# Seven sparse hops on one core: blocks gathered and scattered in pairs, fetches in fours, token scaling on ScalarE

## The chip, the core and the metric

One core of a Trainium2 chip runs the whole program. Its engines work side by side, each through its own queue in order, and wait for each other on semaphores: TensorE (PE in the profile, its weight loads PEld) for matrix products into PSUM, VectorE (DVE) and ScalarE (ACT) for elementwise work and for copies out of PSUM, GpSimd (POOL), which here mostly issues gathers by index from memory, and SyncE (SP), which issues plain transfers. The metric is the device time of one execution in microseconds. The kernel before takes 3991.62 us (median of 3 runs, 3988.89 to 3995.74).

## What is computed

A graph with 10,000 nodes, 160,000 edges and rows of 128 numbers. Seven hops each sum, for every node, the scaled rows of its neighbours; the eight rows that a node then has (its own and one of each hop) go through a small attention layer.

```python
h = x
toks = [x]
for _ in range(7):
    msg = h[src] * deg_inv_sqrt[src, None] * deg_inv_sqrt[dst, None]
    h = _segment_sum(msg, dst, N)
    toks.append(h)
tok = jnp.stack(toks, axis=1)                      # (N, 8, D)
...
return jnp.einsum('nk,nkd->nd', alpha, o)
```

The change lies in hops 2 to 7. The sorting of the edges, hop 1 and the attention keep their code.

## The kernel before

**Tables.** The rows of a hop stand in SBUF as a table `tab` of 80 tiles of 128 nodes, each row in two halves of fp16 (a value and its remainder, 256 columns together). There are two such tables, and hops read one and write the other. The written rows also go to memory (`tabd`, and `tabh` for tiles 72 to 78), because a part of the edges is fetched from there.

**Blocks.** The nodes that receive are cut into 79 tiles; the work for one is a block. What it needs of the edges was made once in hop 1: a matrix `w` of 128 x 4736 fp8 ones and zeros, which every hop loads again from memory (`GSd`, line 695, on SP). Its columns are 72 gather matrices of 32 columns, 18 scatter matrices of 128 columns and one matrix for fetched rows. Tiles 72 to 78 come first in a hop, then 0 to 71 (`order`).

**Gather (`gather`, lines 533 to 543).** A tile `p` in PSUM takes eight matmuls (line 539): 32 columns of `w` against one tile of the table each, so that four of them, on four groups of 32 columns of the array, make 128 rows of 256 sums. Nine such tiles, jj = 0 to 8, make a block. A copy (line 542) brings each as fp16 into a buffer `eb`: ScalarE copies jj = 0, 2, 4, 5, 7, VectorE 1, 3, 6, 8 (`evac`). The pool of `p` has six banks (`pg2`), and there are 14 buffers `eb`.

**Scatter (`scat`, lines 510 to 519).** Two matmuls per tile (line 515), 128 columns of `w` against a buffer `eb`, add up into the block's accumulator `acc` (two banks, `pc2`). The scatter of a tile is put into a list, `pend`, and taken from it later: after the nine gathers of a block, `begin` (lines 505 to 508) opens the new accumulator with two matmuls on fetched rows (line 501), and the list is run down to two entries (`lag`). So TensorE's order is: nine gathers of block n, `begin` of n, the last two scatters of n - 1 and its `close`, seven scatters of n, nine gathers of n + 1.

**End of a block (`close`, `fin`).** VectorE sums the accumulator's two halves into `s` (line 530). ScalarE scales it into the new table (672), VectorE makes the remainder (673) and the row's largest value (675), ScalarE's queue issues the write of the new rows to `tabd` (158), and for tiles 72 to 78 to `tabh` (162). `token_out` scales `s` into the output `r`, in hop 1 on ScalarE (566), in the later hops on GpSimd (568), and SP writes it (570).

**Fetches (`fetch`, lines 483 to 488).** The edges that the gather's slots don't hold come as rows by index: two tiles `og` of 128 rows for each block, one from `tabh` (index 0) and one from `tabd` (index `NI` = 1), each an indirect transfer that GpSimd issues. `ahead(n)` fetches for block n + 2. The pool has two buffers for each index. For the first two blocks of a hop the rows from `tabd` (named `ogl`) can be fetched only when the old hop's last rows have landed; these blocks (`late`) take them in `close` (528).

**Who sets the order.** The program is written as the loops below; a scheduler puts each engine's instructions into a fixed order when the program is built, and the order of TensorE follows the text. Block 0 of a hop also computes the hop's scale (`mid`, lines 659 to 668).

Of the kernel before, what the change touches and what calls it, by code (L numbers as in the profile page):

```python
# [12 lines left out]
AF = mybir.ActivationFunctionType  # L13
ALU = mybir.AluOpType
# [23 lines left out]
class Hops:  # L38
# [441 lines left out]
            yield  # L480


    def fetch(self, t, i, src, name=None):

        o = self.ogp.tile([128, 256], F16, name=name or f"og{i}", bufs=2 if name else None)
        self.nc.gpsimd.indirect_dma_start(out=o, out_offset=None, in_=src[0] if i == NI else src[1],  # L486
                                          in_offset=bass.IndirectOffsetOnAxis(ap=self.oidx[:, t, i:i + 1], axis=0))
        return o

    def block(self, t, w, tab, og, pend, lag, runs, first, evac, fin, lead=False, late=False, mid=None, ahead=None):  # L490

        nc, V, A, T, G = self.nc, self.nc.vector, self.nc.scalar, self.nc.tensor, self.nc.gpsimd
        m = 257 if first else 256
        acc = []


        def fetched(i, start=False, stop=False):
            W = w[:, (NG + i) * 128:(NG + i + 1) * 128] if i < NI else self.Sov[:, t, :]  # L500
            T.matmul(acc[0][:, :256], W, og[i], start=start, stop=stop)  # L501
            if first:
                T.matmul(acc[0][:, 256:257], W, self.ones16, start=False, stop=False)

        def begin():
            acc.append(self.pacc.tile([128, 512], F32, name="acc", tag="acc"))
            for i in range(NI if late else NI + 1):
                fetched(i, start=i == 0)

        def scat(e, jj):  # L510
            if not acc:
                acc.append(self.pacc.tile([128, 512], F32, name="acc", tag="acc"))
            for j in range(e.shape[1]):
                J = 2 * jj + j
                T.matmul(acc[0][:, :m], w[:, J * 128:(J + 1) * 128], e[:, j, :m], start=first and J == 0,  # L515
                         stop=J == NG - 1 and not (first or late))
                if first and J == 0 and not lead:
                    for i in range(NI):
                        fetched(i)

        def close():
            if first:
                if lead:
                    for i in range(NI):
                        fetched(i)
                T.matmul(acc[0][:, 256:257], self.Sov[:, t, :], self.ones16, start=False, stop=False)
            if first or late:
                T.matmul(acc[0][:, :256], self.Sov[:, t, :], og[NI], start=False, stop=True)  # L528
            s = self.fp.tile([128, 128], F32, name="s")
            V.tensor_reduce(s, acc[0][:, 0:256].rearrange("p (h d) -> p d h", h=2), axis=X, op=ALU.add)  # L530
            fin(t, s, acc[0])

        def gather(jj):
            n = min(2, NG - 2 * jj)
            p = self.pg.tile([128, 2, 2, 128], F32, name="p")
            for j in range(n):
                for q in range(4):
                    s = 4 * (2 * jj + j) + q
                    T.matmul(p[32 * q:32 * q + 32, j], w[:, NJ * 128 + s * CAP:NJ * 128 + (s + 1) * CAP], tab[:, s, :], start=True, stop=True)  # L539
            e = self.ebuf[self.eb_i % len(self.ebuf)]  # L540
            self.eb_i += 1
            (A.copy if evac(jj) else V.tensor_copy)(e[:, :n, 0:256], p[:, :n].rearrange("p j h d -> p j (h d)"))  # L542
            pend.append(lambda: scat(e[:, :n], jj))

        jj = 0
        for i, n in enumerate(runs):
            for _ in range(n):
                gather(jj)
                jj += 1
            if mid:  # L550
                mid(0)
            if not first:
                begin()
                ahead()
            while len(pend) > lag:
                pend.pop(0)()
            if mid:
                mid(1)
            if i == len(runs) - 1:
                pend.append(close)  # L560
            yield

    def token_out(self, k, t, s, ct):
        r = self.fp.tile([128, 128], F32, name="r")
        if k == 1:
            self.nc.scalar.activation(r, s, AF.Copy, scale=ct[:, t:t + 1])
        else:
            self.nc.gpsimd.tensor_scalar(r, s, ct[:, t:t + 1], None, op0=ALU.mult)  # L568
        n = min(128, N - t * 128)
        self.nc.sync.dma_start(self.tok[k][t * 128:t * 128 + n, :], r[:n])  # L570

    def run(self, ctx, nhop=K):
# [54 lines left out]
        if nhop == 1:  # L627
            return
        with ExitStack() as c:
            self.gsp = c.enter_context(tc.tile_pool(name="gs2", bufs=5))  # L630
            self.pg = c.enter_context(tc.tile_pool(name="pg2", bufs=6, space=PSUM))
            self.pacc = c.enter_context(tc.tile_pool(name="pc2", bufs=2, space=PSUM))
            self.ogp = c.enter_context(tc.tile_pool(name="og2", bufs=2))
            self.fp = c.enter_context(tc.tile_pool(name="fp2", bufs=4))
            self.sp = c.enter_context(tc.tile_pool(name="sp2", bufs=2))
            self.more_ebufs(c.enter_context(tc.tile_pool(name="eb2", bufs=1)), 9)

            mc = self.sp.tile([128, 1], F32, name="mc")
            V.tensor_reduce(mc, self.mx[0], axis=X, op=ALU.max)
# [10 lines left out]
            for k in range(2, nhop + 1):  # L650
                i = k % 2
                tab, new = self.tab[i], self.tab[1 - i]
                din = self.tabd[1 - i], self.tabh[1 - i]
                ct, c1, mx, mo = self.ctok[i], self.c1[i], self.mx[i], self.mx[1 - i]
                last = k == nhop
                V.tensor_scalar(ct, self.disT, self.sinv, None, op0=ALU.mult)


                def scale(part, c1=c1, mx=mx):
                    if part == 0:  # L660
                        mc = self.sp.tile([128, 1], F32, name="mc")
                        V.tensor_reduce(mc, mx, axis=X, op=ALU.max)
                        V.tensor_mul(mc, mc, self.rho)
                        scale.m = self.colmax(self.pg, self.sp, mc, "p")
                    else:
                        q = self.pow2_of(self.pg, self.sp, scale.m, 2.0 ** 8, "p")
                        V.tensor_mul(self.sinv, self.sinv, q[:, 1:2])
                        V.tensor_scalar(c1, self.dis2, q[:, 0:1], None, op0=ALU.mult)

                def fin(t, s, acc, k=k, ct=ct, c1=c1, mo=mo, new=new, last=last, i=i):  # L670
                    if not last:
                        A.activation(new[:, t, 0:128], s, AF.Copy, scale=c1[:, t:t + 1])  # L672
                        V.scalar_tensor_tensor(new[:, t, 128:256], s, c1[:, t:t + 1], new[:, t, 0:128],  # L673
                                               op0=ALU.mult, op1=ALU.subtract)
                        V.tensor_reduce(mo[:, t:t + 1], new[:, t, 0:128], axis=X, op=ALU.max, apply_absolute_value=True)
                        self.rows(i, new, t, t + 1, nc.scalar)
                    self.token_out(k, t, s, ct)


                order = [*range(4 * NG, NT), *range(4 * NG)]  # L680
                og = [[None] * (NI + 1) for _ in order]


                def ahead(n, og=og, order=order, din=din):
                    if n + 2 < NT:
                        for j in range(NI):
                            og[n + 2][j] = self.fetch(order[n + 2], j, din)
                    for m in range(0 if n == 0 else n + 2, min(n + 3, NT) if n >= 0 else 0):
                        og[m][NI] = self.fetch(order[m], NI, din, "ogl" if m < 2 else None)

                ahead(-2)
                ahead(-1)
                for n, t in enumerate(order):
                    w = self.gsp.tile([128, (NJ + NG) * 128], F8, name="w")
                    nc.sync.dma_start(w, self.GSd[t])
                    for _ in self.block(t, w, tab, og[n], pend, 2, (9,), False, lambda jj: jj in (0, 2, 4, 5, 7), fin, n == 0, n < 2,
                                        scale if n == 0 and not last else None, lambda n=n: ahead(n)):
                        pass
                while pend:
                    pend.pop(0)()  # L700

# [502 lines left out]
```

## Time and profile before

| what | value |
|---|---|
| median of 3 runs | 3991.62 us (3988.89 to 3995.74) |
| the profiled execution | 3991.25 us, its span 3989.5 us |
| mean granted clock of TensorE | 0.973 |
| TensorE busy | 3698.0 us (93%), 69691 matmuls |
| VectorE, ScalarE, GpSimd busy | 3307.7 us (83%), 2652.1 us (66%), 1683.4 us (42%) |
| hops 2 to 7 | from about 1170 to 3290 us |

Times in the profile are microseconds from the span's start unless marked ns. A row of the timeline has the start, the length, the engine (a q behind it marks an instruction of the engine's queue, such as the issue of a transfer), the line, the operation, what it writes and reads, and the count of merged instructions; in brackets stands the engine's idle time just before, and what ended it. A matmul's recorded length holds the passage through the array, so that neighbours overlap: how fast matmuls follow is read from their starts. A row of the list of waits has who waited for whom, the sum in us, how often, and the longest. A row of the groups has line, engine, operation, shapes, count, then the busy us and the mean ns of one, and the idle time before it. A row of the windows has the window, its length, the busy us of PE, PEld, DVE, ACT and POOL with counts, the granted clock, the share of the DMA engines and GB/s.

### The profile page before, as it was taken

The page shows a single profiled execution, that of the slowest core. Times are in us where ns is not written, and L with a number is a line of the kernel's source. Part 1 is how long each engine was busy: PE and PEld are TensorE (multiplying, and loading weights), DVE is VectorE, ACT ScalarE, POOL GpSimd, SP SyncE. Part 2 cuts the span into 40 slices and gives each one's busy share as a digit, 9 for nine tenths or more (in the row PEclk, how much of TensorE's full clock was granted, in tenths as well). Part 3 has the DMA queues.
Part 4 walks back from the last instruction along what each step waited for, and adds up shares of the span by engine and source line. Part 5 has one row for each costly group of instructions (what it writes and reads, how often), then busy time and mean ns, then how long its engine had stood idle before and what let it go on. Part 6 is the DMA issues. An engine that isn't in the chain of part 4 may idle for free.

```text
span 3989.5 us, 163466 instructions
## 1 busy us (share of the span) xinstructions
PE 3698.0 (93%) x69691; PEld 3031.0 (76%) x69691; DVE 3307.7 (83%) x6948; ACT 2652.1 (66%) x6799; POOL 1683.4 (42%) x1898
## 2 busy tenths in 40 slices
PE   4776799999979999999999999999999997999997
PEld 3765666667648888888888888888888886888885
DVE  8999999999967777777777777777766665999998
ACT  6774366666666666666666666666655557888884
POOL 0000333334335555555555555555555551222222
PEclk8888999999989999999999999999999998999998
DMA  3100345445456666666666666666655553222220
GB/s 107 30 1 1 128 151 159 144 152 155 148 177 193 202 203 198 201 199 207 193 203 200 193 204 202 200 196 202 202 186 185 186 168 91 76 79 77 74 74 13
DMA packets 320617, 594.82 MB, mean 149 GB/s; under 512 B 55624, under 2 KB 213542, under 8 KB 314630
## 3 DMA queue, kind: packets, MB, share of 16 engines
q1 hardware_dynamic: 219749, 477.37, 37.7%
q0 software_dynamic: 35392, 72.55, 5.9%
q10 hardware_dynamic: 64736, 34.38, 3.0%
q8 instruction: 546, 8.95, 0.9%
q14 instruction: 194, 1.58, 0.1%
HBM read 455.43 MB, written 128.67 MB: 146 GB/s over the span
## 4 chain that ended last, share of the span: by engine, by line
PE 64%; DVE 2%; DMA 2%; ACT 1%; issue 1%; POOL 0%; ACTq 0%; SPq 0%; POOLq 0%; DVEq 0%
PE p L539 24%; PE acc L515 23%; PE acc L501 4%; PE pv L888 3%; PE po L899 3%; PE pu L877 3%; PE pt L867 2%; PE ps L919 1%; PE pf L1067 1%; PE sm L925 1%; DMA og<-tabh,oidx 1%; DMA tabd<-tab 0%; ACT junk L913 0%; DVE st L994 0%; DVE o L905 0%
## 5 line engine op out<-in xcount | busy, mean ns | idle before, releaser
L542 ACT CAST eb<-p 128x512 f16<-128x512 f32 x3081 | 1591.3, 603 | 672.5 <-PE p L539 647.3
L542 DVE CAST eb<-p 128x512 f16<-128x512 f32 x1896 | 1179.3, 683 | 345.0 <-PE p L539 329.6
L539 PE MATMUL p<-tab,w 128*32 128x256 f16 x39816 | 1284.0, 274 | 39.1 <-ACT eb L542 21.9
L515 PE MATMUL acc<-eb,w 128*128 128x256 f16 (+1 forms) x9954 | 1240.5, 274 | 12.1 <-DVE indeg L590 9.5
L539 PEld LDWEIGHTS <-w 128*32 128x32 fp8e4 x39816 | 1002.6, 97 | 237.6 <-issue 180.6
L486 POOL DMA_INDIRECT og<-tabh,oidx x553 | 632.5, 1144 | 1253.5 <-PE acc L501 658.7
L515 PEld LDWEIGHTS <-w 128*128 128x128 fp8e4 x9954 | 951.6, 98 | 176.9 <-issue 62.5
L486 POOL DMA_INDIRECT og<-tabd,oidx x541 | 560.9, 1037 | 444.7 <-PE acc L528 262.7
L568 POOL TENSOR_SCALAR r<-s,ctok 128x128 f32<-128x128 f32 x474 | 297.1, 627 | 27.4 <-DVE s L530 13.4
L672 ACT ACTIVATE tab<-s,c 128x128 f16<-128x128 f32 x395 | 158.6, 401 | 202.5 <-DVE s L530 202.5
L673 DVE SCALAR_TENSOR_TENSOR tab<-s,c,tab 128x128 f16<-128x128 f32 x395 | 140.1, 355 | 183.0 <-ACT tab L672 182.9
L315 ACT ACTIVATE o<-oh,d2s 128x79 f16<-128x79 f16 x800 | 204.6, 373 | 81.0 <-PE ta L329 81.0
L530 DVE TENSOR_REDUCE s<-acc 128x128 f32<-128x256 f32 x553 | 229.3, 415 | 28.6 <-PE acc L528 23.8
L913 ACT ACTIVATE junk<-x 128x128 f32<-128x128 f32 x625 | 245.0, 394 | 0.0
L476 DVE TENSOR_TENSOR w<-dsl,iof 128x2432 fp8e4<-128x2432 f16 x79 | 211.8, 2681 | 0.0
L899 PEld LDWEIGHTS po<-v,pT 128*128 128x128 f32 x1250 | 159.1, 193 | 44.7 <-issue 27.6
L329 PE MATMUL ta<-o,ro 128*128 128x158 f16 x1250 | 119.7, 267 | 77.9 <-DVE ro L325 77.9
L971 POOL TENSOR_TENSOR p<-e,in 128x512 f32<-128x512 f32 (+1 forms) x40 | 40.8, 1019 | 343.0 <-DVE e L969 343.0
L888 PE MATMUL pv<-Wv,xT 128*128 128x131 f32 x1250 | 176.0, 284 | 4.5 <-ACT xT L868 3.7
L329 PEld LDWEIGHTS <-ro 128*128 128x128 f16 x1250 | 114.4, 113 | 82.2 <-DVE ro L325 82.1
L899 PE MATMUL po<-v,pT 128*128 128x128 f32 x1250 | 166.9, 277 | 7.7 <-DVE o L905 7.7
L888 PEld LDWEIGHTS pv<-Wv,xT 128*128 128x128 f32 x1250 | 153.3, 192 | 21.2 <-issue 8.2
(276 smaller groups left out, 4489.1 us busy)
## 6 DMA issues: line engine op xcount, KB each, us to landing
w<-gsd SPq DMA_DIRECT2D x474, 592.0 KB
gsd<-w SPq DMA_DIRECT2D x79, 592.0 KB
rb<-srow SPq DMA_DIRECT2D x79, 576.0 KB
tok<-r SPq DMA_DIRECT2D x546, 64.0 KB
x<-tok SPq DMA_DIRECT2D x266, 128.0 KB
tabd<-tab ACTq DMA_DIRECT2D x395, 64.0 KB
og<-tabh,oidx POOLq DMA_INDIRECT x553
og<-tabd,oidx POOLq DMA_INDIRECT x541
```

Of the source, the lines that this page charges most:

```text
L315: A.activation(o[:, j - a, NK:, i], oh[:, j, :, i], AF.Copy, scale=d2s[:, c0:c0 + 1])
L329: T.matmul(ta, ro[:, j - a, :, i], o[:, j - a, :, i], start=j + i == 0, stop=j + i == NP)
L476: V.tensor_tensor(w[:, :NJ * 128].rearrange("p (j d) -> p j d", d=128), dsl[:, g, :, None].to_broadcast([128, NJ, 128]), self.iof1[:, None ...
L486: self.nc.gpsimd.indirect_dma_start(out=o, out_offset=None, in_=src[0] if i == NI else src[1], in_offset=bass.IndirectOffsetOnAxis(ap=self ...
L515: T.matmul(acc[0][:, :m], w[:, J * 128:(J + 1) * 128], e[:, j, :m], start=first and J == 0, stop=J == NG - 1 and not (first or late))
L530: V.tensor_reduce(s, acc[0][:, 0:256].rearrange("p (h d) -> p d h", h=2), axis=X, op=ALU.add)
L539: T.matmul(p[32 * q:32 * q + 32, j], w[:, NJ * 128 + s * CAP:NJ * 128 + (s + 1) * CAP], tab[:, s, :], start=True, stop=True)
L542: (A.copy if evac(jj) else V.tensor_copy)(e[:, :n, 0:256], p[:, :n].rearrange("p j h d -> p j (h d)"))
L568: self.nc.gpsimd.tensor_scalar(r, s, ct[:, t:t + 1], None, op0=ALU.mult)
L888: T.matmul(p[:, g - a, :], S[i]["xT"][:, g, :], Wv, start=True, stop=True)
L899: T.matmul(p[:, g - a, :], PT[i % 2][:, g, :], S[i]["v"][:, g, :128], start=True, stop=True)
L913: A.activation(j, S[i]["x"][:, g, :], AF.Square, bias=S[i]["x"][:, g, 0:1], scale=-1.0, accum_out=S[i]["sq"][:, g:g + 1])
```

## The change

After block 0 of a hop, the remaining 78 blocks go in 39 pairs. In a pair the first block's nine gathers are followed by the second's nine; then `begin` of the first, the two scatters left over from the pair before with its `close`, all nine scatters of the first block and its `close` at once (`behind`), `begin` of the second and seven of its scatters. The loads of `w` of both blocks are issued together at the pair's start, from six buffers instead of five. The buffers `eb` grow from 14 to 21, those of `og` from two to four for each index. The four fetches of the pair after next are issued one after the other, behind a GpSimd copy of one column (`tensor_copy` in `fetch`) that reads the buffer of the second block's first copy and writes into the first fetch's tile, so that none of them is issued before that copy is done. In block 0 the fetches stand where they stood, except in hop 7, where they are held until the copy of jj = 4. `r` is computed on ScalarE in all hops.

```diff
-    def fetch(self, t, i, src, name=None):
+    def fetch(self, t, i, src, name=None, after=None):
         o = self.ogp.tile([128, 256], F16, name=name or f"og{i}", bufs=2 if name else None)
+        if after is not None:
+            self.nc.gpsimd.tensor_copy(o[:, 0:1], after)
         self.nc.gpsimd.indirect_dma_start(out=o, out_offset=None, in_=src[0] if i == NI else src[1],
...
             for _ in range(n):
                 gather(jj)
+                if jj == (4 if lone else 0) and not first and not mid and not behind:
+                    ahead(self.ebuf[(self.eb_i - 1) % len(self.ebuf)][:, 0, 0:1])
                 jj += 1
+            if not first:
+                yield
             if mid:
                 mid(0)
             if not first:
                 begin()
-                ahead()
-            while len(pend) > lag:
+                if mid:
+                    ahead()
+            while len(pend) > (behind or lag):
                 pend.pop(0)()
             if mid:
                 mid(1)
-            if i == len(runs) - 1:
+            if behind:
+                close()
+            elif i == len(runs) - 1:
                 pend.append(close)
             yield
...
         r = self.fp.tile([128, 128], F32, name="r")
-        if k == 1:
-            self.nc.scalar.activation(r, s, AF.Copy, scale=ct[:, t:t + 1])
-        else:
-            self.nc.gpsimd.tensor_scalar(r, s, ct[:, t:t + 1], None, op0=ALU.mult)
+        self.nc.scalar.activation(r, s, AF.Copy, scale=ct[:, t:t + 1])
...
-            self.gsp = c.enter_context(tc.tile_pool(name="gs2", bufs=5))
+            self.gsp = c.enter_context(tc.tile_pool(name="gs2", bufs=6))
...
-            self.ogp = c.enter_context(tc.tile_pool(name="og2", bufs=2))
+            self.ogp = c.enter_context(tc.tile_pool(name="og2", bufs=4))
...
-            self.more_ebufs(c.enter_context(tc.tile_pool(name="eb2", bufs=1)), 9)
+            self.more_ebufs(c.enter_context(tc.tile_pool(name="eb2", bufs=1)), 16)
...
-                for n, t in enumerate(order):
+                def start(n, **kw):
                     w = self.gsp.tile([128, (NJ + NG) * 128], F8, name="w")
-                    nc.sync.dma_start(w, self.GSd[t])
-                    for _ in self.block(t, w, tab, og[n], pend, 2, (9,), False, lambda jj: jj in (0, 2, 4, 5, 7), fin, n == 0, n < 2,
-                                        scale if n == 0 and not last else None, lambda n=n: ahead(n)):
-                        pass
+                    nc.sync.dma_start(w, self.GSd[order[n]])
+                    return self.block(order[n], w, tab, og[n], pend, 2, (9,), False, lambda jj: jj in (0, 2, 4, 5, 7), fin, n == 0, n < 2,
+                                      scale if n == 0 and not last else None, **kw)
+
+                for _ in start(0, ahead=lambda after=None: ahead(0, after)):
+                    pass
+
+                for n in range(1, NT, 2):
+                    two = (start(n, behind=9),
+                           start(n + 1, lone=False, ahead=lambda after, n=n: (ahead(n, after), ahead(n + 1))))
+                    for _ in range(2):
+                        for g in two:
+                            next(g)
```

More of the change, by code (lines that the diff above doesn't have):

```diff
@@ L488, in fetch, with block @@
         return o
-    def block(self, t, w, tab, og, pend, lag, runs, first, evac, fin, lead=False, late=False, mid=None, ahead=None):
+    def block(self, t, w, tab, og, pend, lag, runs, first, evac, fin, lead=False, late=False, mid=None, ahead=None, behind=0, lone=True):
         nc, V, A, T, G = self.nc, self.nc.vector, self.nc.scalar, self.nc.tensor, self.nc.gpsimd
@@ L681, in run, with ahead @@
                 og = [[None] * (NI + 1) for _ in order]
-                def ahead(n, og=og, order=order, din=din):
+                def ahead(n, after=None, og=og, order=order, din=din):
                     if n + 2 < NT:
                         for j in range(NI):
-                            og[n + 2][j] = self.fetch(order[n + 2], j, din)
+                            og[n + 2][j] = self.fetch(order[n + 2], j, din, after=after)
                     for m in range(0 if n == 0 else n + 2, min(n + 3, NT) if n >= 0 else 0):
```

## The prediction

> **What bounds the kernel now.** I read the chain of waits first, then the windows, then the timeline of hops 2 to 7, then the list of who waits for whom.
>
> ```profile
> span 3989.5 us, 163466 instructions
> ...
> PE p L539 24%; PE acc L515 23%; PE acc L501 4%; PE pv L888 3%; PE po L899 3%; PE pu L877 3%; PE pt L867 2%; PE ps L919 1%; PE pf L1067 1%; PE sm L925 1%; DMA og<-tabh,oidx 1%; DMA tabd<-tab 0%; ACT junk L913 0%; DVE st L994 0%; DVE o L905 0%
> ```
> ```profile
> 400.00:800.00 400.00, 360.46 (x6443) 270.39 (x6441) 394.96 (x577) 224.58 (x495) 145.04 (x80) 0.97 0.46 146
> ...
> 2000.00:2400.00 400.00, 396.80 (x8310) 334.72 (x8312) 306.30 (x644) 265.17 (x541) 233.06 (x271) 1.00 0.63 200
> ```
>
> TensorE's gather (L539) and scatter (L515, L501) carry half of the chain, and in the hops (second window; columns PE, PEld, DVE, ACT, POOL, clock) TensorE is busy 396.80 of 400 us at clock 1.00, VectorE 306 and ScalarE 265. One block, and where the next begins:
>
> ```profile
> 2000.57 1.87 PEld L539 LDWEIGHTS <-w 128*32 128x32 fp8e4 x72 [0.21 <-issue]
> 2000.58 2.15 PE L539 MATMUL p<-tab,w 128*32 128x256 f16 x72
> 2001.03 2.54 ACT L542 CAST eb<-p 128x512 f16<-128x512 f32 x5 [0.90 <-PE p L539]
> ...
> 2001.25 2.48 DVE L542 CAST eb<-p 128x512 f16<-128x512 f32 x4 [0.54 <-PE p L539]
> ...
> 2002.65 0.10 PEld L501 LDWEIGHTS <-w 128*128 128x128 fp8e4 x1 [0.21 <-issue]
> 2002.66 0.28 PE L501 MATMUL acc<-og,w 128*128 128x256 f16 x1
> ...
> 2002.89 2.13 PE L515 MATMUL acc<-eb,w 128*128 128x256 f16 x18
> 2003.22 1.01 POOL L486 DMA_INDIRECT og<-tabh,oidx  x1 [1.45 <-PE acc L501]
> ...
> 2003.65 0.41 DVE L530 TENSOR_REDUCE s<-acc 128x128 f32<-128x256 f32 x1
> 2004.10 0.40 ACT L672 ACTIVATE tab<-s,c 128x128 f16<-128x128 f32 x1 [0.52 <-DVE s L530]
> 2004.53 0.94 POOL L486 DMA_INDIRECT og<-tabd,oidx  x1 [0.30 <-issue]
> 2004.53 0.35 DVE L673 SCALAR_TENSOR_TENSOR tab<-s,c,tab 128x128 f16<-128x128 f32 x1 [0.47 <-ACT tab L672]
> 2004.80 0.28 DVE L675 TENSOR_REDUCE mx<-tab 128x1 f32<-128x128 f16 x1
> 2004.92 0.33 ACTq L158 DMA_DIRECT2D tabd<-tab  x1
> ...
> 2005.40 0.58 ACT L542 CAST eb<-p 128x512 f16<-128x512 f32 x1 [0.90 <-PE p L539]
> 2005.62 0.69 DVE L542 CAST eb<-p 128x512 f16<-128x512 f32 x1 [0.54 <-PE p L539]
> ...
> 2026.78 0.95 PE L539 MATMUL p<-tab,w 128*32 128x256 f16 x28
> ```
>
> From 2000.58 to 2026.78 are six blocks: 4.367 us each. A scatter matmul takes one step of (2.13 - 0.27)/17 = 0.109 us (0.27 is one matmul's recorded length), and four gather matmuls, on 32 columns each, share a step: 18 steps of gather and 20 of scatter are 4.15. The other 0.217 falls on the two changes between 32 and 128 columns, where the weight load idles 0.21 for "issue", about half of it beyond a normal step. These are nearly all of such idle time:
>
> ```profile
> PEld L501 <- issue: 98.8, 468, 0.2
> PEld L539 <- issue: 93.4, 434, 1.2
> ...
> PE acc L528 <- DMA ogl<-tabd,oidx: 8.8, 5, 3.7
> ```
>
> **The change part by part.** *Two gathers in a row, then two scatters.* A pair has two changes of columns instead of four: -0.217 us. But the nine tiles p of a block (eight matmuls, two steps, 0.218 us each) go through six banks, and each is emptied by a copy (L542), on ScalarE for jj 0, 2, 4, 5, 7 and on VectorE for 1, 3, 6, 8. ScalarE ends a copy every (2.54 - 0.58)/4 = 0.49 us, VectorE every (2.48 - 0.69)/3 = 0.597: together one tile per 0.269, slower than the 0.218 at which TensorE makes them. Nine tiles fit, since six banks lie ahead; eighteen do not. When a full bank gives TensorE its work back is seen at a hop's start, where an issue of tabh held ScalarE:
>
> ```profile
> 1907.85 0.82 ACTq L162 DMA_DIRECT2D tabh<-tab  x1
> ...
> 1908.71 0.58 ACT L542 CAST eb<-p 128x512 f16<-128x512 f32 x1 [1.65 <-PE p L539]
> ...
> 1909.35 0.89 PE L539 MATMUL p<-tab,w 128*32 128x256 f16 x24 [0.23 <-ACT eb L542]
> ```
>
> The copy ends at 1909.29 or 1909.30, the gather goes on 0.05 later. So, from a pair's first gather matmul on, the first copies end at 0.45 + 0.58 = 1.03 (ScalarE) and 0.67 + 0.69 = 1.36 (VectorE), and tile k waits for the copy of tile k - 6:
> - k = 9 (would start 1.96): VectorE's 2nd copy, 1.36 + 0.60 + 0.05 = 2.01: 0.05 late.
> - k = 11 (now 2.45): ScalarE's 4th, 1.03 + 3 x 0.49 + 0.05 = 2.55: 0.10.
> - k = 13 (2.99): ScalarE's 5th, 3.04: 0.05. k = 15 (3.48): its 6th, 3.53: 0.05. k = 16 (3.75): VectorE's 5th, 1.36 + 4 x 0.597 + 0.05 = 3.80: 0.05. The others don't wait.
>
> Sum 0.30 us a pair, so a pair loses 0.30 - 0.217 = 0.083. With 39 pairs in 6 hops: 234 x 0.083 = **+19.4 us**. Bounds: the bank free at the copy's end (no 0.05) leaves 0.25, +8 us; VectorE 2% slower, 0.61 a copy (an allowance of mine: no row has eight of its copies in a row), makes it 0.35, +31 us.
>
> *Hop starts.* Tile 0's last matmul (L528) waits for the fetch ogl:
>
> ```profile
> 1896.65 2.37 PE L539 MATMUL p<-tab,w 128*32 128x256 f16 x72
> ...
> 1897.19 0.94 POOL L486 DMA_INDIRECT ogl<-tabd,oidx  x1 [2.56 <-DMA tabd<-tab]
> ...
> 1897.67 2.48 DVE L542 CAST eb<-p 128x512 f16<-128x512 f32 x4
> ...
> 1898.44 0.94 POOL L486 DMA_INDIRECT ogl<-tabd,oidx  x1 [0.30 <-issue]
> ...
> 1899.69 0.95 POOL L486 DMA_INDIRECT og<-tabd,oidx  x1 [0.30 <-issue]
> ...
> 1901.16 0.27 PE L528 MATMUL acc<-ogl,Sov 128*128 128x256 f16 x1 [1.92 <-DMA ogl<-tabd,oidx]
> ```
>
> Now the gather of a second block stands ahead of it, some 2.2 us. Of the 8.8 us (5 times, longest 3.7) all but 3.7 - 2.2 = 1.5 goes: **-7.3 us**. What is late next is og of tile 2, issued 1899.69 and by ogl's 3.97 us landed at 1903.66; TensorE comes for it at 1896.65 + 4.25 (two gathers) + 0.11 + 24 x 0.109 = 1903.63: nothing, to 1 us a hop.
>
> *Token scaling on ScalarE.* Its cost stands in hop 1, and what it replaces on the page:
>
> ```profile
> 1152.55 0.40 ACT L591 ACTIVATE tab<-s,dis 128x128 f32<-128x128 f32 x1
> ...
> 1152.85 0.39 ACT L566 ACTIVATE r<-s,ctok 128x128 f32<-128x128 f32 x1
> ```
> ```profile
> L568 POOL TENSOR_SCALAR r<-s,ctok 128x128 f32<-128x128 f32 x474 | 297.1, 627 | 27.4 <-DVE s L530 13.4
> ```
>
> It starts 0.30 after tab and takes 0.39. In the built order ScalarE does ten copies, then twice tab, r, issue of tabd. The second block of the pair before closes first: VectorE's 8th copy ends at 1.36 + 7 x 0.597 = 5.54, then s, tab, r, issue are over by 7.06. This pair's first block closes after 4.25 + 0.11 + 24 x 0.109 = 6.98; by the distances of the rows above s runs 7.19 to 7.60, tab to 8.04, r to 8.33, L673 to 8.43, the issue to 8.79. The next pair starts at 8.82 and its first copy is ready at 9.27. So r is covered by L673, which the issue awaits anyway, and 0.48 us are left: **0 us**; without this cover each 0.1 us beyond it costs 234 x 0.1 = 23 us. POOL loses 474 x 0.627 us, which nothing waited for.
>
> *Four fetches in a row, held.* The hold is a copy of 128x1 on POOL, which no row shows: above nothing, below a memset of 128x520:
>
> ```profile
> 1162.17 4.31 POOL L117 MEMSET eb<- 128x520 f16 x9 [9.33 <-PE acc L526]
> ```
>
> that is under 0.48 us; I take 0.1, as it is 1/520 of that size. It waits for ScalarE's 6th copy (1.03 + 5 x 0.49 = 3.48), and behind it on POOL stand the four fetches, 1.25 us apart as ogl above: the last is issued at 7.4 and by ogl's 3.97 lands at 11.4; the first use is at 8.82 + 4.36 = 13.18. **0 us**, with 1.8 to spare. Their issues now fall together with VectorE's last copies; the row at 1897.67 has four copies under two fetches in 2.48 us, as in a block without. [...]
>
> *Loads and buffers.* The loads of w stand on SP among the token writes, which now wait for ScalarE's r:
>
> ```profile
> 1165.83 0.80 SPq L695 DMA_DIRECT2D w<-gsd  x2
> ...
> 1169.89 1.79 PE L539 MATMUL p<-tab,w 128*32 128x256 f16 x20 [3.72 <-DMA w<-gsd]
> ...
> 2003.52 0.32 SPq L695 DMA_DIRECT2D w<-gsd  x1
> ```
>
> One takes about 4 us (the first gather waits from its issue to 1169.89). Today it is issued 14.5 us ahead: 2003.52, in the block from 2000.58, for the block four later. With six buffers a pair's second load goes out when the write of the second token two pairs earlier has its r, 6.6 into that pair, and is needed 2 us into its own: 2 x 8.82 + 2.0 - 6.6 = 13 us ahead, the first one more. Seven more memsets take POOL 3.4 us at the start of hop 2, long before ogl. **0 us**.
>
> Sum, against the profiled execution's own 3991.25 us (span 3989.5, the median of the runs 3991.62): 3991.25 + 19.4 - 7.3 = **4003 us**. Its own range, from the bounds (+8 to +33, -7.3, hop starts 0 to +6): 3992 to 4021.
>
> **The rivals.**
> 1. *The banks come free in time*: a copy lets go of its bank earlier than its recorded end, and the stall is a third or none. For it: steady blocks show no such stall. Against: 1909.35. With 0.10: 234 x (0.10 - 0.217) - 7 = -34, 3957; with none 3933; with 0.18: 3975.
> 2. *ScalarE's tail reaches the next pair*, on the slow side: the last s of a pair is 0.7 us late, as when one of the four fetches (0.95 us) holds up VectorE's last copies, or r doesn't hide. It decides beyond 0.48 us: 0.22 x 234 = +51 on the 4003, 4054. Against: the 0.48 of slack, and 1897.67.
> 3. *The change doesn't halve the 0.217*: the idle "issue" belongs to the first matmul on a new accumulator, not to the columns, and stays four times a pair. Then only the stall is left: 234 x 0.30 - 7 = +63, 4054. For it: the load at 2002.65 is also a new accumulator's. Against: L539 has the same 0.21 with no accumulator.
> 4. *The clock falls*: hop 1, where gather and scatter change places every two tiles, runs at 0.97 (first window above). At 0.97 the hops' 474 x 4.367 = 2070 us cost 62 more: 4065. [...]
>
> **How the numbers follow.** Chances: forecast 0.60, rival 1 0.19, rival 2 0.09, rival 3 0.08, rival 4 0.04. The range takes the forecast's whole 3992 to 4021, rival 1 down to 3965 and rivals 2 and 3 at 4054, less some of their ends: **3965 to 4055**. A measurement of this kernel tells about 0.2% (8 us) from no change. Faster by that: rival 1, nearly all, and 0.01 of the forecast: 0.20. Within it: 0.18 of the forecast, whose lower third ends at 4000. Slower: the rest, 0.41 + 0.21 = 0.62. The 4003 is the likeliest case's.
>
> **What would show it.** A pair's period: 8.82 us (8.73 now for two blocks; 8.52 would be rival 1). Its 144 gather matmuls from first to last start: 4.14 us, not 3.83; the stalls of 0.05 to 0.10 hide under the recorded 0.27 of a matmul, so that few rows of idle PE will name "eb". "PEld L501 <- issue" should fall to about half its 468 times (else rival 3); ScalarE's first copy should start 0.45 after the pair's first gather (else rival 2); the clock stays 1.00 (else 4); L528's wait falls from 8.8 to some 1.5. I would be wrong if tiles after the ninth start in step.

## The result, and the profile after

The changed kernel takes 4047.54 us (median of 4 runs, 4043.94 to 4056.35), the kernel before, beside it, 3992.59 us (3988.89 to 3995.74): ratio 1.0136, 95% interval 1.0124 to 1.0147. That is 55 us slower, where 12 were forecast: the direction and the range (3965 to 4055) hold, the 4003 doesn't. The profiled execution took 4047.05 us. Its span, from the page, and the hops' window (columns as before: TensorE, its weight loads, VectorE, ScalarE, GpSimd, clock):

```profile
span 4045.3 us, 162825 instructions
```
```profile
2000.00:2400.00 400.00, 390.86 (x8043) 329.87 (x8035) 296.12 (x623) 278.86 (x613) 177.76 (x218) 1.00 0.67 193
```

The clock is 1.00, as before; TensorE does 8043 matmuls in the 400 us instead of 8310, 3.2% fewer. One pair in the timeline:

```profile
2032.73 2.44 PEld L542 LDWEIGHTS <-w 128*32 128x32 fp8e4 x89 [0.21 <-issue]
2032.74 4.48 PE L542 MATMUL p<-tab,w 128*32 128x256 f16 x144
2033.24 4.99 ACT L545 CAST eb<-p 128x512 f16<-128x512 f32 x10 [0.99 <-PE p L542]
2033.41 4.87 DVE L545 CAST eb<-p 128x512 f16<-128x512 f32 x8 [0.87 <-PE p L542]
2035.35 1.59 PEld L542 LDWEIGHTS <-w 128*32 128x32 fp8e4 x55 [0.18 <-issue]
2036.34 0.18 POOL L487 COPY og<-eb 128x1 f16<-128x1 f16 x1 [3.73 <-ACT eb L545]
2036.68 0.98 POOL L488 DMA_INDIRECT og<-tabh,oidx  x1 [0.15 <-issue]
...
2037.15 0.28 PE L504 MATMUL acc<-og,w 128*128 128x256 f16 x1
...
2041.26 0.33 ACTq L158 DMA_DIRECT2D tabd<-tab  x1
2041.62 0.67 PEld L542 LDWEIGHTS <-w 128*32 128x32 fp8e4 x28 [0.21 <-issue]
```

The pair lasts from 2032.74 to 2041.62, 8.88 us; some 170 of the 234 pairs take 8.89 or 8.90. Two single blocks were 8.735. The weight loads run in step for 89 matmuls, just past the eleventh tile, and idle 0.18 there; in e9, where ScalarE's ten copies take 3.87 us instead of 4.99, all 144 run in step, in 3.83. ScalarE's first copy starts 0.50 after the first gather; before it was 0.45. The tail is off the path: ScalarE's last issue ends at 2041.59, and the next first copy starts at 2042.13.

Who waits for whom in the hops (sum, times, longest), and under it the rows of the kernel before for the fetched rows:

```profile
PEld L542 <- issue: 100.9, 460, 1.5
PEld L504 <- issue: 47.5, 223, 0.4
...
PE acc L518 <- issue: 11.3, 14, 1.9
PE acc L504 <- DMA og<-tabh,oidx: 10.9, 5, 4.8
...
PE p L542 <- issue: 4.8, 8, 1.2
...
PE acc L504 <- DMA og<-tabd,oidx: 1.8, 1, 1.8
```
```profile
PE acc L501 <- DMA og<-tabh,oidx: 3.5, 1, 3.5
...
PE acc L501 <- DMA og<-tabd,oidx: 0.4, 2, 0.2
```

The idle time ahead of `begin` (L504; L501 before) has halved. The wait for ogl is gone. In its place TensorE waits for og once at each hop's start, 10.9 us at five and 1.8 at the sixth. The longest of these, 4.8 in hop 2, is mostly not new: 3.5 of it stand in the kernel before. So og takes 12.7 us instead of 3.9, some 9 more. New is that TensorE stops 22 times with no wait on any semaphore (the rows of L518 and L542). One such stop, TensorE alone:

```profile
2099.81 0.38 PE L518 MATMUL acc<-eb,w 128*128 128x256 f16 x2
2102.12 2.12 PE L518 MATMUL acc<-eb,w 128*128 128x256 f16 x18 [1.93 <-issue]
```

By the starts of matmuls the hops have 27 places where the next one comes more than 0.33 us after the one ahead without a wait; together they lose 21 us. The kernel before has none. They don't lie anywhere: nearly all begin 4.2 to 6.7 us after a pair's first gather, at its last tile or in the scatter behind it. The trace's list of DMA packets shows what they go with: 26 of the 27 end 2.2 to 3.1 us after the start of a packet of 16,384 bytes on the queue that the page lists as "q8 instruction". There are 546 such packets in the run, and 139,382 matmuls and weight loads: some 255 to a packet. Counted in these instructions, each of the 26 stands 428 to 436 behind 256 times the number of the packet that it ends after (both counted from 0); with 255 or 257 for the 256 they would spread over some 300. I read the stops as TensorE out of its own instructions until that packet was in.

The wait for og stands at the hops' starts, here that of hop 4:

```profile
1929.87 0.94 POOL L488 DMA_INDIRECT og<-tabd,oidx  x1 [0.30 <-PE acc L518]
...
1930.82 0.19 POOL L487 COPY og<-eb 128x1 f16<-128x1 f16 x1
1931.16 0.97 POOL L488 DMA_INDIRECT og<-tabh,oidx  x1 [0.15 <-issue]
...
1932.44 0.95 POOL L488 DMA_INDIRECT og<-tabh,oidx  x1 [0.30 <-issue]
...
1937.63 0.28 PE L504 MATMUL acc<-og,w 128*128 128x256 f16 x1 [1.17 <-DMA og<-tabh,oidx]
```

GpSimd is busy with the six fetches that the old hop's last rows let go until 1930.81; only then come the hold and the fetches for tiles 3 and 4, whose `begin` stands waiting at 1937.63.

The 55.8 us between the spans, read from this profile: 234 pairs x 0.15 = +35, the stops +21, og at the hops' starts +9, ogl -9: +56. The experiments take the 35 apart and test the rest.

### The profile page after: what moved, and what is told of

Read it like the earlier page. It is cut to its first block, busy times and chain, and to the rows that moved or that the text cites. A ratio compares the mean times of both kernels' runs of the same rounds, so it can differ in the third digit from the quotient of the medians.

```text
span 4045.3 us, 162825 instructions
## 1 busy us (share of the span) xinstructions
PE 3737.6 (92%) x69691; PEld 3067.7 (76%) x69691; DVE 3305.2 (82%) x6948; ACT 2776.9 (69%) x7273; POOL 1420.4 (35%) x1660
## 5 line engine op out<-in xcount | busy, mean ns | idle before, releaser
L545 ACT CAST eb<-p 128x512 f16<-128x512 f32 x3081 | 1569.4, 625 | 410.9 <-PE p L542 402.9
L545 DVE CAST eb<-p 128x512 f16<-128x512 f32 x1896 | 1158.0, 680 | 262.1 <-PE p L542 261.0
L542 PE MATMUL p<-tab,w 128*32 128x256 f16 x39816 | 1328.2, 275 | 46.2 <-ACT eb L545 23.4
L518 PE MATMUL acc<-eb,w 128*128 128x256 f16 (+1 forms) x9954 | 1242.0, 273 | 22.9 <-issue 11.3
L542 PEld LDWEIGHTS <-w 128*32 128x32 fp8e4 x39816 | 1016.6, 96 | 291.8 <-issue 186.4
L518 PEld LDWEIGHTS <-w 128*128 128x128 fp8e4 x9954 | 952.6, 98 | 183.6 <-issue 71.1
L488 POOL DMA_INDIRECT og<-tabh,oidx x553 | 609.2, 1102 | 703.8 <-DVE vi L440 401.6
L488 POOL DMA_INDIRECT og<-tabd,oidx x541 | 571.9, 1057 | 471.2 <-PE acc L531 274.0
L487 POOL COPY og<-eb 128x1 f16<-128x1 f16 x229 | 42.6, 186 | 830.8 <-ACT eb L545 830.8
L575 ACT ACTIVATE r<-s,ctok 128x128 f32<-128x128 f32 x553 | 214.9, 389 | 75.4 <-DVE s L533 74.1
```

## The experiments

In the first four runs (e1 to e4, on one chip) the kernel before took 4234.41 us, in all others (e5 to e8 on a second chip, e9 to e11 on a third) 3995; ratios are to the kernel before beside each run.

**e1, no hold** (and e7, the same kernel).

```diff
-        if after is not None:
-            self.nc.gpsimd.tensor_copy(o[:, 0:1], after)
```

> The changed kernel without the 128x1 copy on GpSimd that holds the four fetches; everything else stays. My account of the changed kernel's +55 us: a steady pair of 8.885 us instead of two blocks of 4.367 (8.735), 234 x 0.15 = +35; 26 stops of TensorE with no wait on a semaphore, about +21; the wait for og at the start of five hops, about +10; the wait for ogl gone, -9. Of the 0.15, 0.05 to 0.07 is put down to the hold: ScalarE's first copy of a pair starts 0.505 after the pair's first gather instead of 0.45, because the queue has one more semaphore to wait for. Without the hold: first copy at 0.45, pair 8.82 to 8.83, no wait for og at the hops' starts: 4047 - 234 x 0.06 - 10 = 4023 us if the 26 stops stay (they come from 288 gather instructions in a row, faster than TensorE's instructions are brought in), 4003 if they go too (they come from the four fetches in a row, which are now issued in twos as buffers come free). Rival: the 0.505 is not the hold's; then pairs stay at 8.88 and only the hop starts go, 4037 or 4016.

Measured 4377.86 us, ratio 1.0345 (1.0328 to 1.0362): a far larger loss than the change itself has in 1.0136, and not one of the ways expected. Pairs take 10.27 us. The timeline shows why:

```profile
2158.11 0.94 POOL L486 DMA_INDIRECT og<-tabd,oidx  x1 [0.30 <-issue]
2158.15 0.66 PEld L540 LDWEIGHTS <-w 128*32 128x32 fp8e4 x27 [0.21 <-issue]
...
2159.93 3.33 PE L540 MATMUL p<-tab,w 128*32 128x256 f16 x93 [0.83 <-issue]
...
2160.05 3.52 ACT L543 CAST eb<-p 128x512 f16<-128x512 f32 x7 [2.38 <-PE p L540]
```

A fetch is issued 0.04 us ahead of the gather; the gather stops after 27 matmuls, and the copies of a tile long done start only 1.90 us after its first matmul. What this says of the hold had to be asked again, in e7.

**e2, token scaling alone.**

```diff
-        if k == 1:
-            self.nc.scalar.activation(r, s, AF.Copy, scale=ct[:, t:t + 1])
-        else:
-            self.nc.gpsimd.tensor_scalar(r, s, ct[:, t:t + 1], None, op0=ALU.mult)
+        self.nc.scalar.activation(r, s, AF.Copy, scale=ct[:, t:t + 1])
```

> The kernel before with the token scaling on ScalarE and nothing else of the change. Account: r lies under VectorE's remainder, nothing waits for it: 3992, within 8 us, blocks of 4.367. Rival (ScalarE's tail): r holds up the issue of tabd and the next block's first copies by up to 0.4 a block; TensorE has no slack for it in nine tiles over six banks beyond about 0.5, so 0.1 to 0.2 a block would be +47 to +95 us.

Measured 4232.07 us, ratio 0.9997 (0.9987 to 1.0007): r costs nothing here. As the time is the same, its profile also stands for the kernel before on this chip, with blocks of 4.85 us:

```profile
2152.88 0.94 POOL L486 DMA_INDIRECT og<-tabd,oidx  x1 [0.30 <-issue]
...
2153.36 2.60 PE L539 MATMUL p<-tab,w 128*32 128x256 f16 x72
...
2154.44 2.05 ACT L542 CAST eb<-p 128x512 f16<-128x512 f32 x4 [1.19 <-PE p L539]
```

Here the fetch starts 0.48 ahead of the gather, and the first copy 1.08 behind it. In the profile before, the same fetch at 2004.53 stood 0.42 ahead of the gather, and the copy at 2005.40 came 0.45 behind it. So what a fetch does to a gather that follows within half a microsecond is not the same in the two groups of runs.

**e3 and e4, half of the copies' columns**, in pairs and in single blocks.

```diff
-            (A.copy if evac(jj) else V.tensor_copy)(e[:, :n, 0:256], p[:, :n].rearrange("p j h d -> p j (h d)"))
+            hw = 256 if first else 128
+            (A.copy if evac(jj) else V.tensor_copy)(e[:, :n, 0:hw], p[:, :n].rearrange("p j h d -> p j (h d)")[:, :, 0:hw])
```

> The changed kernel, in hops 2 to 7 with copies out of PSUM of the first 128 columns only; the remainder half of the gathered rows is left out (the scatter reads old values there, with the same matmuls). A copy of half the columns takes less than 0.3 on ScalarE and about 0.35 on VectorE (an estimate: half of 0.49 and 0.60, with something fixed), together one tile per 0.17, faster than the 0.218 of TensorE. If the pair's excess is the six banks: no stall, the gather from first to last start 3.83 instead of 4.21, pair 8.52, 4047 - 234 x 0.365 = 3962 us, and less if the hops' starts gain too. The stops without a wait stay or grow (the gather is denser). If the excess lies elsewhere (ScalarE's tail, the hold, the changes of columns), pair above 8.7 and the time above 4000.

> The kernel before, in hops 2 to 7 with copies out of PSUM of the first 128 columns only (the remainder half of the gathered rows is left out): the other side of the comparison with the pairs. TensorE sets the block, its banks come free in time already: 4.367 a block and 3992 us, a few us less at the hops' starts. Then the pair's gain in the changes of columns alone is two blocks here less one pair of the half copies, 8.735 - 8.52 = 0.217. If blocks get shorter here, the copies bound the kernel before as well, and my account of its 4.367 falls.

Measured e3 4122.53 us, 0.9744 (0.9728 to 0.9761), and e4 4102.54, 0.9693 (0.9677 to 0.9709). In e3 the gather runs in step, 3.84 us from first to last start, which speaks for the banks; but its pairs take 9.07 us in the median: now the scatter stops while fetches are issued (idle time ahead of L518, for no wait: 203 us, against 71 in the changed kernel's first profile). e4 got faster, against its expectation. Both mix the copies with the fetches here and decide nothing of the sum; e9 and e11 repeat the question without that.

**e5, the changed kernel again**, as the measure for e6 and e7.

> The changed kernel itself, as the measure for the kernels that run beside it. In the runs with e1 to e4 the kernel before took 4234 us instead of 3992: every block was 4.85 us instead of 4.367, and its first copies came 1.10 us after its first gather instead of 0.46, where a fetch on GpSimd had been issued less than half a microsecond ahead of that gather (without a fetch so near: 0.45). In the changed kernel the held fetches stand in the middle of the pair, away from its first gather. So, where the kernel before takes about 3992, the changed one takes 4047 again; where it takes about 4234, the pair escapes that delay at its start and meets the fetches elsewhere in its gather or scatter: pair 9.2 to 9.6 us instead of 9.70 for two blocks, 4120 to 4210 us. If the hold has nothing to do with that delay: about 4290.

Measured 4053.45 us beside 3995.26: 1.0148 (1.0132 to 1.0163), the first result again. What it would be where the kernel before takes 4234 stays open.

**e6, no fetches.**

```diff
+        if self.fixed is not None:
+            if after is not None:
+                self.nc.gpsimd.tensor_copy(self.ogp.tile([128, 1], F16, name="hold", bufs=4), after)
+            return self.fixed
...
```

> The changed kernel with the fetched rows left out in hops 2 to 7: two matmuls of a block read a fixed tile of zeros instead, GpSimd's hold copy goes to a scratch tile, no indirect transfer is issued there. If TensorE's stops without a wait come from 288 gather instructions in a row (instructions brought in too slowly), they stay at their place just after the 18th tile, about 25 of them and 20 us; if they come from the four fetches in a row, they go. In both cases the waits for og at the hops' starts go (10 us), the banks' stall stays 0.375 and a pair 8.88: 4035 us with the stops, 4015 without, whatever the time of the kernel before is, since all fetches near the gathers are gone too.

Measured 4010.24 us, 1.0035 (1.0022 to 1.0049), 43 us less than e5. Pairs still take 8.89. The stops are all but gone:

```profile
PE acc L520 <- issue: 0.5, 2, 0.3
```

So most of them need the fetches: without, a gather of this length leaves six short ones, 1.9 us by the starts of matmuls, and four of these stand at that place of a block. The pair's 8.89, the hold still in it, has nothing to do with fetches.

**e7, no hold, beside e5.**

> The changed kernel without the hold, beside the changed kernel. As for e1: where the kernel before takes about 3992, ScalarE's first copy 0.45 after the pair's first gather, banks' stall 0.32 instead of 0.375, pair 8.82 to 8.83, hop starts 10 us better, 4023 us. Where it takes about 4234: 4378 as in e1, since the fetches then fall on the pair's first gathers, and the difference to the changed kernel is what the hold is worth there.

Measured 4033.09 us, 1.0098 (1.0083 to 1.0114), 20 us less than e5.

```profile
2051.68 0.94 POOL L486 DMA_INDIRECT og<-tabd,oidx  x1 [0.30 <-issue]
2051.72 4.43 PE L540 MATMUL p<-tab,w 128*32 128x256 f16 x144
2052.18 4.99 ACT L543 CAST eb<-p 128x512 f16<-128x512 f32 x10 [0.94 <-DVE mx L680]
...
2056.08 0.28 PE L502 MATMUL acc<-og,w 128*128 128x256 f16 x1
...
2060.55 4.43 PE L540 MATMUL p<-tab,w 128*32 128x256 f16 x144
```

The first copy starts 0.46 after the first gather, and the pair takes 8.83 us: the hold costs 0.054 a pair, though it runs on GpSimd. That holds in hops 2 to 6, 195 pairs, 10.5 us. In hop 7 a pair takes 8.90 with the hold and without: there VectorE's first copy starts 0.74 after the first gather instead of 0.67, in the kernel before too. In the changed kernel's records ScalarE does 11 instructions at L545 in such a pair instead of 10: an extra one of 17 ns at 0.45 precedes the first copy, whose wait list names GpSimd's semaphore beside TensorE's. It is a buffer `eb` that a hold has read and this copy overwrites. Counted through 21 buffers and 18 tiles a pair, that buffer comes to VectorE on its next turn (the sixth copy of the next pair, which has the wait too) and to ScalarE on its third, some 32 us after the hold. The event is long past. The kernel before has no such instruction ahead of its first copy, at 0.45; so I put the 0.054 down to that one instruction more. Of the other 10 us nearly 9 are the hops' starts: four of the five waits for og<-tabh are gone, hop 2's is left. The stops stay (26, 20.5 us), although the fetches are issued in twos and 1 us later: 4.92, 6.17, 7.54 and 8.79 us after a pair's first gather in the median, instead of 3.95, 5.23, 6.48 and 7.82.

**e8, only the first pair of a hop**, single blocks from tile 3 on, no hold, r on GpSimd.

```diff
...
+                two = start(1, behind=9, ahead=lambda: ahead(1)), start(2, ahead=lambda: ahead(2))
+                for _ in range(2):
+                    for g in two:
+                        next(g)
+                for n in range(3, NT):
+                    for _ in start(n, ahead=lambda n=n: ahead(n)):
+                        pass
```

> The kernel before, with only blocks 1 and 2 of each hop as a pair (gathered in a row, then scattered), single blocks from 3 on, no hold, token scaling on GpSimd, four buffers og for each index, six for w. By my account the pair hides the wait for ogl (8.8 us over five hops) at the price of one pair's stall less two column changes (6 x 0.1): 3992 - 8 = 3984 us, 0.2% faster than before, if og of tile 2 isn't late next; if it is, by the 1 us a hop or more, 3990 and no difference.

Measured 3989.36 us, 0.9986 (0.9977 to 0.9995): 6 us below the kernel before and 64 below the changed one. The pair hides ogl where it pays (8.8 us of waiting is down to 2.0), no other pair pays for banks, and TensorE never stops for want of instructions.

**e9, the pair by itself**, and **e11**, its other side (the kernel of e4).

> The pair by itself: the changed kernel in hops 2 to 7 with copies of the first 128 columns only (the remainder half of the gathered rows is left out), no fetched rows (a fixed tile of zeros instead) and no hold. If a pair's price is the six banks and its gain the two changes of columns saved, the gather of 144 runs in step (first to last start 3.83 us) and a pair takes 8.735 - 0.217 = 8.52 us: 234 x 0.215 = 50 less than single blocks, and 9 to 12 less at the hops' starts: about 3935 us, where the kernel before takes 3995. The stops without a wait: none to a few, since there are no fetches. If the accumulators and not the columns cost the 0.217: pair 8.73 and 3983 us.

> The kernel before with copies of the first 128 columns only (the remainder half left out), beside e9 on one chip. Where the kernel before takes about 3995, its blocks stay at 4.367 and the time within 8 us: copies don't bound single blocks, so e9's gain is the pair's. If blocks get shorter, the copies bound them too.

Measured e9 3919.36 us, 0.9814 (0.9798 to 0.9831), and e11 3992.20, 0.9993 (0.9983 to 1.0003), with blocks of 4.37. e9's timeline:

```profile
2052.49 3.83 PEld L542 LDWEIGHTS <-w 128*32 128x32 fp8e4 x144 [0.21 <-issue]
2052.49 4.11 PE L542 MATMUL p<-tab,w 128*32 128x256 f16 x144
2052.95 3.87 ACT L546 CAST eb<-p 128x256 f16<-128x256 f32 x10 [0.94 <-PE p L542]
...
2061.01 1.17 PE L542 MATMUL p<-tab,w 128*32 128x256 f16 x36
```

The pair takes 8.52 us, as worked out: with faster copies the stall is gone, and what a pair saves in changes of columns is 8.735 - 8.52 = 0.215. Against e11 the time is 73 us lower; 50 are the pairs. e11 keeps its fetches, and its TensorE waits 15.5 us for them at the hops' starts, which e9 doesn't; the rest was not traced further.

e9 also shows more of the stops. It has no fetch, but its gather is denser (3.84 us from first to last start instead of 4.21), and ten stops are back, 4.9 us by the starts of matmuls. Density alone makes some.

**e10, the hold seven tiles later.**

```diff
-                if jj == (4 if lone else 0) and not first and not mid and not behind:
+                if jj == (4 if lone else 7) and not first and not mid and not behind:
```

> The changed kernel with the hold on the 17th tile's copy instead of the 10th's: the four fetches are issued from some 5.5 us after a pair's first gather, in its scatter, instead of from 1.7 us on. TensorE's stops without a wait follow a packet of its instructions that lands 2.4 to 4.9 us after a pair's first gather. If fetches under way in just that time make these packets late, the stops go: about 20 us less in the steady pairs (left: 5 us at most, as without fetches), while the held fetches of the hops' starts come 3.3 us later, 5 x 3.3 = 16 us more: 4053 - 20 + 16 = 4049 us, with pairs at 8.83 to 8.89. If the gather's density alone or fetches anywhere in the pair make the stops, there are some 25 of them as before and the time is 4065 to 4070.

Measured 4034.99 us, 1.0101 (1.0084 to 1.0118), 18 us less than e5. Pairs take 8.90: ScalarE's first copy is back at 0.45, but the hold's wait now stands ahead of VectorE's first copy (0.74 instead of 0.67) and ScalarE's third. The timeline of a pair, and the rows of stops in the hops:

```profile
2107.39 4.50 PE L542 MATMUL p<-tab,w 128*32 128x256 f16 x144
...
2112.90 0.18 POOL L487 COPY og<-eb 128x1 f16<-128x1 f16 x1 [3.84 <-ACT eb L545]
...
2113.24 0.98 POOL L488 DMA_INDIRECT og<-tabh,oidx  x1 [0.15 <-issue]
```

```profile
PE acc L504 <- DMA og<-tabh,oidx: 10.6, 5, 5.1
...
PE p L542 <- issue: 1.5, 5, 0.5
PE acc L518 <- issue: 1.2, 3, 0.6
```

By matmul starts the stops fall from 23 (21.8 us, e5) to 10 (4.5 us): 17 of the 18 us. All that has moved is the hold and, behind it, the four fetches, issued 5.85, 7.13 and 8.38 us after the pair's first gather and 0.73 into the next pair, 1.9 us later than in the changed kernel (where the first is issued at 3.95, not at the 1.7 of the expectation). So when the fetches are issued decides over most of the stops.

The packets show it too. Packets of instructions, numbered n from 0, start at the earliest when TensorE has started some 144 instructions more than 256 n. From that moment on, packet n starts after (us, packets between 1300 and 3200 of the span):

| kernel | median | 95% of packets within |
|---|---|---|
| before | 1.2 | 2.0 |
| e6, no fetches | 1.2 | 2.5 |
| e9, no fetches, denser gather | 1.2 | 2.8 |
| the changed kernel | 2.0 | 4.6 |
| e7, no hold | 2.0 | 4.5 |
| e10, fetches later | 1.7 | 3.3 |

What in a fetch makes them late is not shown. It isn't simply a transfer that runs beside them. Most packets start 3.0 to 4.4 us after a pair's first gather, and there 2.7 packets of the fetches' queue are under way on average in e10 and 1.1 in the changed kernel. The hops' starts did not get worse by the 16 us that I had put on them.

## Why the forecast was right in sign and short in size

- *Two changes of columns saved, -0.217 a pair*: right. e9 shows 0.215, and the idle time ahead of `begin` halved from 99 to 47.5 us. Rival 3 falls.
- *Six banks, +0.30 a pair, so +0.083*: right, tile by tile. In e7's median pair of hops 2 to 6 the tiles k = 9, 11, 13, 15 and 16 start 0.04, 0.11, 0.05, 0.06 and 0.05 late, 0.31 in all, and no other does. A pair is 8.83 there, +0.098, against the 8.82 predicted. In hop 7 it is 8.90, +0.163: the prediction put hop 4's rows on all six hops. Together 195 x 0.098 + 39 x 0.163 = +25.5 us against +19.4. Rival 1 falls: tiles 9 and 11 start 0.05 after the row of their copy ends.
- *ogl, -7.3*: right in kind, 8.8 in size; the row is gone. But og takes as much: the fetched rows are waited for 12.7 us in all, before and after.
- *Token scaling on ScalarE, 0*: right: e2 shows it for single blocks, on the chip of e1 to e4. Rival 2 falls: in the changed kernel 0.54 us are left at the end of the pair.
- *Loads of w and buffers, 0*: no new wait for w appears.
- *The gather's length*: 4.16 us from first to last start in e7, 4.14 predicted; 4.21 in the changed kernel, with the hold's 0.06.
- *VectorE under the fetches*: eight copies in 4.87 us, 0.60 each, with a fetch at 2036.68 beside them; the kernel before has 0.597, so no copy waits for the fetch, as the prediction's row had it.
- *The clock*: 1.00 in the hops' window from 2000 to 2400, in the kernel before and in the changed one; rival 4 falls.
- *Four fetches in a row, held, 0 with 1.8 to spare*: this is the step that failed, by some 40 us in three parts. First, the hold was priced as work of GpSimd (0.18 us, indeed covered), but it reads a buffer that ScalarE writes later, and the added semaphore delays ScalarE's first copy by 0.054 in the very stretch where banks are short: 10.5 us (e7). Second, the slack of 1.8 was that of a steady pair; at a hop's start the hold stands on GpSimd behind six other fetches, and og is waited for 9 us longer in all. Some 6 of them, in hops 3 to 6, go with the hold (e7); the rest, in hops 2 and 7, is there without it. Third, TensorE's own instructions were taken as always there: 21 us of stops.

For the third, both kernels take 546 packets of 16,384 bytes, 256 of TensorE's instructions to each by the count above; the kernel before has no stop with them, the changed one 26. In the changed kernel a pair's gather is 288 instructions (144 matmuls and 144 weight loads) in 4.2 us, 256 in 3.7 us, where two single blocks have a scatter of 2.2 us between their 144s; and with the fetches one packet in twenty starts over 4.6 us behind the mark above, against 2.0 before.

The terms again: +25.5 banks less columns, +10.5 the hold's semaphore, +21 stops, +9 og, -9 ogl: +57 against 55.8 between the spans. The 4003 was the first and the last of these alone. That the range held is luck: its upper end came from rivals that priced other mechanisms at about the same sum.

Open: what in a fetch makes the instruction packets late; the runs show that leaving the fetches out or issuing them later removes most of it. Whether four fetches in a row are worse than twos at the same place was not tried; e7's twos, 1 us later, make as many stops.

## What to carry to other kernels

A hold that is free on its own engine can still cost on another: ask which engines will later overwrite the data that it reads, and add that wait to their queues; here it cost 0.054 us each time, though the hold was over some 32 us before. Slack found in the steady state says nothing of the first round of a loop, where the same queue is full of other work: here 1.8 us to spare in the pair, and some 6 us of waiting at the hops' starts that go with the hold. Joining two short dense stretches into a long one saves the changes between them (0.215 us a pair in e9), but look at what each stretch draws on meanwhile, buffers to drain into and instructions alike; try other places for the transfers beside it, or join only where a wait is hidden, as e8 does.

## What was not expected of the hardware

The same kernel took 3995 us in some runs and 4234 in others, 6%, at the same granted clock (0.97 each). The difference lies in the hops and in one pattern: in e1 to e4, where GpSimd issues a fetch 0.48 us ahead of a gather's first matmul, the first copies start 1.08 us after that matmul instead of 0.45 (e2); where it is issued 0.04 ahead (e1), 1.90. The copies of both engines are late together, and TensorE stops in the same stretch. In the other runs the same order of instructions shows none of it (e7: fetch 0.04 ahead, copy after 0.46). All of e1 to e4 ran on one chip, the others on two more, each group at its own time; so the pattern goes with that chip or that time, and what it is isn't shown. A place for fetches that is free in one can be dear in the other: the same kernel without the hold is 1.0% slower than the one before in e7 and 3.4% in e1.
